# Attention feeding a PReLU layer on one Trainium2 core: the output weights loaded in eight pieces, one small load put later, the work between two blocks re-ordered

## The chip, the cores and the metric

The kernel runs on one core of one Trainium2 chip. The metric is the device time in microseconds (us) of one execution. The profile also gives the span from the first to the last instruction on the core, which is somewhat shorter than the device time: in the profiled execution of the kernel before, the device time was 279.78 us and the span 278.0 us.

Five engines work side by side and wait for each other through semaphores: TensorE (PE in the profile; its weight loads are PEld), VectorE (DVE), ScalarE (ACT), GpSimd (POOL) and SyncE (SP). Loads and stores are DMAs which an engine issues and which run on their own.

## The reference, cut to what matters

Eight batches of 576 tokens, eight heads of 64 features. The attention has no softmax; it is followed by a normalisation over each head's 64 features, and then by two matrix products with a PReLU between them, over all 4608 tokens.

```python
# q, k, v: (8 batches, 8 heads, 576 tokens, 64); w_in: (512, 2048); w_out: (2048, 512)
kv  = einsum('bhsd,bhse->bhde', k, v)
o   = einsum('bhsd,bhde->bhse', q, kv)
rms = sqrt(mean(o * o, axis=-1, keepdims=True) + 1e-06)
x   = (o / rms * g_norm)            # laid out as (4608 tokens, 512)
h   = x @ w_in
g   = maximum(h, 0) + alpha * minimum(h, 0)
out = g @ w_out                     # float32
```

## The kernel before

The tokens are worked on in nine blocks of 512 (`w` = 0 to 8). A batch has 576 tokens, so block 1 takes the last 64 tokens of batch 0 and the first 448 of batch 1, and block 2 the last 128 of batch 1 and the first 384 of batch 2.

A block's first product is made in 16 groups of 128 hidden features. Each group is four matmuls of 512 columns into one PSUM bank; ScalarE (`m_sb`) and VectorE (`gt`) read the bank, and only then can another group write it. The second product of block 0 is made directly, in 64 matmuls of 512 columns (`y_mm`: four token tiles `a`, sixteen feature groups `g`). From block 1 on it is made from seven products of half-sized matrices instead of eight, in 112 matmuls of 256 columns; it needs sums of parts of w_out (`w_sum`) and of the activations (`s_sum`), which VectorE makes.

The attention of the next block is woven into the current one. The stretch between the last group of block 0 and the first of block 1 is called stage two here: it holds most of block 0's second product, the attention of batch 1, and the sums of w_out.

```python
    def load_rem(b, nm):                      # the last 64 tokens of a batch
        nc.gpsimd.dma_start(out=buf_of(b, nm)[0:REM, 0 if nm == "v" else TPP, :, :],
                            in_=srcs[nm][b, :, MAIN:S, :].rearrange("h s d -> s h d"))
    # load_main(b, nm): the first 512 tokens into a stage tile; regroup() copies them to bufs
    def load_batch(b, names=("k", "v", "q")):
        for nm in names:
            load_rem(b, nm)
            load_main(b, nm)
    ...
    def load_w_out(i):                        # i = 0..3, 512 rows of w_out each
        t = w_p.tile([P, GW, D_MODEL], FP16, name=f"w_out_sb{i}")
        nc.gpsimd.dma_start(
            out=t[:], in_=moe_w_out[i*GW*P : (i+1)*GW*P, :].rearrange("(g p) m -> p g m", p=P))
    ...
    for i in range(len(IN_CUTS) - 1):
        load_w_in(i)
    load_batch(1, ("k",))
    load_w_out(0)
    load_batch(1, ("q",))
    load_w_out(1)
    load_batch(1, ("v",))
    load_w_out(2)
    load_w_out(3)
    ...
    # step_t: transposes of q (5 matmuls a pair of heads, then one copy to qt_sb by ScalarE)
    # step_kv: k'v of a pair (5 matmuls, then kv_sb by VectorE)
    # step_ot: q.kv of a pair and its square (ScalarE);  ssq_mm: sum of squares (PE), then
    #          the reciprocal root (ScalarE);  norm: xt (VectorE), the input of the next block
    ...
    load_batch(2, ("q", "k", "v"))
    ... # first three groups of block 0
    for g in range(3, NF):
        m1_group(0, g, {3: S_POOL, 4: O_POOL, 5: O_POOL, 6: Q_POOL}.get(g))
        if g == 14:
            regroup(1, "k", 0, H)
            for nm in ("k", "q"):
                nc.vector.memset(bufs[0][nm][REM:P, TPP, :, :], 0.0)
            for t in qt_sb:
                nc.vector.memset(t[:, :, 0:PAD], 0.0)
                nc.vector.memset(t[:, :, PAD + S : PAD + S + PAD], 0.0)
    ys = {}     # a = 3 in the bank of ps_y, a = 2, 0, 1 in the banks h0, h1, h2 of the groups
    ...
    regroup(1, "q", 0, H)
    for a in (3, 2, 0, 1):
        y_run(a, range(0, 4))
    w_sum(1, 0)
    for j, pool in enumerate((S_POOL, Q_POOL, O_POOL, O_POOL)):
        step_t(1, j, pool)
    for a in (2, 0, 1):
        y_run(a, range(4, 8))
    w_sum(1, 1)
    step_kv(1, 0)
    step_kv(1, 1, Q_POOL)
    ... # the rest of stage two; see the diff
    store_engines[0] = (nc.sync,)
    ...
    QT_AT = {False: {7: (0, 1), 9: (2, 3), 11: (4,)}, True: {8: (0,), 10: (1,), 12: (2, 3, 4)}}

    def attention(w, u):        # woven into block w - 1, after its group u
        if W_ROW <= w < NW:     # W_ROW = 3
            for what, j in ATT_ROW[w == W_ROW].get(u, ()):
                if what != "kv" or w < B:
                    ROWS[what](w, j)          # "norm" ends with a DMA transpose x_rows -> xt on SP
            if w + 1 < B:
                dma_t(w + 1, QT_AT[w == W_ROW].get(u, ()))   # DMA transposes of q on SP
        ... # blocks 0 to 2 by ATT_1 and ATT_AT
```

Of the kernel before, what the change touches and what calls it, by code (L numbers as in the profile page):

```python
# [10 lines left out]
FP16 = mybir.dt.float16  # L11
# [6 lines left out]
def kernel(  # L18
# [11 lines left out]
    nc = tc.nc  # L30

    B, H, S, D = q.shape
# [3 lines left out]
    P = 128  # L36
# [70 lines left out]
    nc.vector.tensor_copy(out=mask16[:], in_=mask32[:])  # L107
    eps_t = const_p.tile([P, 1], FP32, name="eps_t")
    nc.vector.memset(eps_t[:], 1e-6)

    alpha_row = ysb_p.tile([P, D_MODEL], FP32, name="y_sb")
    nc.sync.dma_start(out=alpha_row[0:NF, 0:P], in_=moe_alpha[:].rearrange("(g p) -> g p", p=P))
# [55 lines left out]
    def regroup(b, nm, h0, h1, eng=None):  # L168
        dst = buf_of(b, nm)[:, 0:TPP, h0:h1, :].rearrange("p t h d -> p h t d")
        src = stages[b, nm][:, h0:h1, :, :]  # L170
        if eng is nc.scalar:
            nc.scalar.copy(out=dst, in_=src)
        else:
            (eng or nc.vector).tensor_copy(out=dst, in_=src)
# [48 lines left out]

    def load_w_out(i):
        t = w_p.tile([P, GW, D_MODEL], FP16, name=f"w_out_sb{i}")
        nc.gpsimd.dma_start(
            out=t[:],
            in_=moe_w_out[i * GW * P : (i + 1) * GW * P, :].rearrange("(g p) m -> p g m", p=P),
        )
        w_out_sb.append(t)  # L230

    def w_in_blk(c, g):
# [41 lines left out]
    def rows(b):  # L274
        return P0 if b == 0 else P

    def n_runs(b):
        return T0 if b == 0 else NT

    def pair_cols(b, nm, j):  # L280
        def f(t):
            n = rows(b)
            if nm == "v" and b == 0:
                h = 2 * j % HH
                return stages[b, nm, 2 * j // HH][0:n, h : h + 2, t, :]
# [7 lines left out]
    def step_t(b, j, pool=(ps_s, "s")):  # L293
        qs = pair_cols(b, "q", j)
        qt_ps = pool[0].tile([P, n_runs(b) * rows(b)], FP16, name="qt_ps", tag=pool[1])
        c = 0
        for t in range(n_runs(b)):
            n = rows(b)
            nc.tensor.matmul(
                out=qt_ps[:, c : c + n],  # L300
                lhsT=qs(t),
                rhs=ident16[0:n, 0:n],
                is_transpose=True,
                start=(t == 0),
                stop=(t == n_runs(b) - 1),
            )
            c += n
        qts[b, j] = qt_sb[b % 2][:, j, PAD : PAD + S]
        if b == 0 and j < 2:
            nc.vector.tensor_copy(out=qts[b, j], in_=qt_ps[:, 0:S])  # L310
        else:
            nc.scalar.copy(out=qts[b, j], in_=qt_ps[:, 0:S])

    PAD = P // 2
    qt_sb = [const_p.tile([P, NPAIR, PAD + S + PAD], FP16, name=f"qt_sb{i}") for i in range(2)]

    def dma_t(b, ts=tuple(range(NT))):
        qt = qt_sb[b % 2][:, :, PAD : PAD + S]
# [435 lines left out]
    h_turn[0] = 2  # L754
    for g in range(3, NF):
        m1_group(0, g, {3: S_POOL, 4: O_POOL, 5: O_POOL, 6: Q_POOL}.get(g))
        if g == 14:
            regroup(1, "k", 0, H)
            for nm in ("k", "q"):
                nc.vector.memset(bufs[0][nm][REM:P, TPP, :, :], 0.0)  # L760
            for t in qt_sb:
                nc.vector.memset(t[:, :, 0:PAD], 0.0)
                nc.vector.memset(t[:, :, PAD + S : PAD + S + PAD], 0.0)


    ys = {}
# [3 lines left out]
    def y_run(a, gs):  # L770
        for g in gs:
            y_mm(ys[a], 0, a, g)
# [9 lines left out]
    w_sum(1, 1)  # L782
    step_kv(1, 0)
    step_kv(1, 1, Q_POOL)
    y_run(3, (4, 5))
    step_kv(1, 2)
    step_kv(1, 3, Q_POOL)
    step_ot(1, 0)
    y_run(3, (6,))
    step_ot(1, 1)  # L790
    y_run(3, (7,))
    y_run(2, (8,))
    ssq_mm(1, 0)
    norm(1, 0)
    y_run(2, (9, 10))
    ssq_mm(1, 1, Q_POOL)
    norm(1, 1)
    w_sum(2, 0)
    w_sum(4, 0)
    y_run(2, (11,))  # L800
    y_run(0, (8, 9, 10))
    step_ot(1, 2)
    y_run(0, (11,))
    y_run(1, (8,))
    step_ot(1, 3)
    y_run(1, (9, 10))
    ssq_mm(1, 2)
    w_sum(2, 1)
    norm(1, 2)
    y_run(1, (11,))  # L810
    y_run(0, (12,))
    ssq_mm(1, 3, Q_POOL)
    norm(1, 3)
    regroup(2, "q", 0, H)
    w_sum(4, 1)
    w_sum(3, 0)
    w_sum(3, 1)
    y_run(0, (13, 14, 15))
    y_out(ys[0], 0, 0)
    y_run(2, range(12, 16))  # L820
    y_out(ys[2], 0, 2)
    y_run(1, range(12, 16))
    y_out(ys[1], 0, 1)
    store_engines[0] = (nc.sync,)
    h_turn[0] = 0
    h_tags[0] = ("h0", "h1", "h2")
# [24 lines left out]
            ATT_AT.setdefault(3 * j + at, []).append((what, j))  # L851
    ATT_1 = {}
    for what, ats in (
        ("t", (0, 2, 4, 7)), ("kv", (4, 5, 6, 8)), ("ot", (7, 7, 11, 12)), ("ssq", (8, 10, 12, 13))
    ):
        for j, at in enumerate(ats):
            ATT_1.setdefault(at, []).append((what, j))
# [35 lines left out]

    REG_AT = {9 + 2 * j: (("k", j),) for j in range(NPAIR)}

    Y3_AT = [(8, 8), (8, 8), (8, 8), (8, 9), (9, 9), (9, 10), (10, 10), (10, 10), (10, 11), (11, 11), (11, 12), (12, 12), (12, 13), (13, 14), (14, 16), (16, 16)]
    REG_2 = {0: (("k", 0), ("k", 1)), 1: (("k", 2), ("k", 3))}

    for w in range(1, NW):
        if w + 2 < B:  # L900
            load_gated(w + 2)
        for u in range(NF):
            if w >= W_ROW - 1 and u in R_FIRST:
                y_read(w - 1, R_FIRST[u])
            m1_group(w, G_ORDER[u])
            if w == W_ROW - 1:
                scale_w_in(G_ORDER[u])
            if w > 1:
# [81 lines left out]
```

## Time and profile before

| | |
|---|---|
| device time, median of 3 runs | 280.06 us (278.78 to 281.0) |
| span of the profiled execution | 278.0 us |
| TensorE busy | 269.5 us, 1928 matmuls |
| VectorE busy | 231.1 us |
| ScalarE busy | 155.6 us |
| one matmul of 512 columns, as profiled | 379 ns |
| granted TensorE clock | 0.999 |

The profile counts an engine as busy from an instruction's start to its end. Matmuls overlap in the array, so their durations do not add up: what a matmul takes of TensorE's time is the distance between one start and the next where nothing is waited for. In the chain view four matmuls of 512 columns take 0.86 us, so one takes 0.216 us; five transposes of 128 columns take 0.28 us, so one takes 0.056 us.

First matmuls of the blocks, from the trace: 15.28 us (block 0), 47.29 (1), 66.80 (2), 95.72 (3), 124.52 (4), 152.81 (5), 180.86 (6), 209.13 (7), 236.06 (8). The last group of block 0 begins at 28.76, the first matmul of block 0's second product at 29.62. Stage two is the stretch from 29.6 to 47.3.

The names in the profile are those of the program's tiles: `vst` and `vsb` are the main part and the last tokens of v, `qst` and `qsb` those of q; `y` is block 0's second product, `yX`, `yY`, `yZ` the later ones; `h_ps` is the first product. A wait such as "PE kv_ps <- DMA vst" says that TensorE stood idle before a matmul into `kv_ps` until a load of `vst` landed.

### The profile page before, as it was taken

Reading aid. Unit: us, or ns where it says so; the run is one execution under the profiler, and the core shown is the slowest. Engines: PE = TensorE matmul, PEld = TensorE weight load, DVE = VectorE, ACT = ScalarE, POOL = GpSimd, SP = SyncE. Lnnn points to the kernel's source line nnn. Section 1 sums busy time; section 2 is a strip of 40 time slices with the busy share of each in tenths; the row PEclk is TensorE's granted clock in tenths of the full one; section 3 lists DMA queues with packets and bytes.
Section 4 is the critical chain, followed back from the end, with each engine's and each line's share of the span. In section 5 each row is a group of like instructions: output and inputs, shape, how many; then the busy total and the mean of one; then the engine's idle time right before and its main releaser. Section 6 shows DMA issues by size and latency. Waiting matters only on the chain.

```text
span 278.0 us, 5178 instructions
## 1 busy us (share of the span) xinstructions
PE 269.5 (97%) x1928; PEld 173.2 (62%) x1928; DVE 231.1 (83%) x446; ACT 155.6 (56%) x284; POOL 81.9 (29%) x115
## 2 busy tenths in 40 slices
PE   7899999999999999999999999999999999999994
PEld 2444454555666676657666766676666666666784
DVE  5669829898789979997899889988998899887862
ACT  3567347789989846654565456545535554444210
POOL 8744432750913346226321831110111011000200
PEclk9999999999999999999999999999999999999999
DMA  8999999999998589986995699520222023201123
GB/s 161 195 207 197 196 203 191 203 136 166 123 170 116 124 112 143 152 184 91 167 186 118 102 167 185 126 78 0 78 75 78 0 77 78 75 0 40 70 84 113
DMA packets 86557, 34.53 MB, mean 124 GB/s; under 512 B 58740, under 2 KB 84868, under 8 KB 86532
## 3 DMA queue, kind: packets, MB, share of 16 engines
q0 software_dynamic: 57424, 24.35, 68.1%
q1 hardware_dynamic: 28212, 8.90, 16.3%
q10 hardware_dynamic: 896, 0.95, 1.1%
q8 instruction: 15, 0.25, 0.4%
q14 instruction: 10, 0.08, 0.1%
HBM read 36.71 MB, written 9.44 MB: 166 GB/s over the span
## 4 chain that ended last, share of the span: by engine, by line
PE 79%; DMA 13%; DVE 4%; issue 2%; ACT 1%; POOL 1%; DVEq 0%; POOLq 0%
PE h_ps L456 37%; PE yY L615 14%; PE yX L615 9%; PE yZ L615 9%; DMA vst<-in_v_dram 5%; DMA w_in_sb<-in_moe_w_in_dram 5%; PE kv_ps L332 3%; PE y L481 2%; DMA qst<-in_q_dram 2%; PE or_ps L398 2%; DVE gt L467 1%; DMA xt<-x_rows 1%; PE ot_ps L354 1%; ACT m_sb L463 1%; PE ssq_ps L370 1%
## 5 line engine op out<-in xcount | busy, mean ns | idle before, releaser
L456 PE MATMUL h_ps<-xt,w_in_sb 128*128 128x512 f16 x576 | 145.2, 379 | 0.8 <-DMA xt<-x_rows 0.6
L463 ACT ACTIVATE m_sb<-h_ps 128x512 f32<-128x512 f32 x144 | 86.1, 598 | 83.5 <-PE h_ps L456 81.9
L467 DVE SCALAR_TENSOR_TENSOR gt<-m_sb,beta_sb,h_ps 128x512 f16<-128x512 f32 x144 | 106.6, 743 | 25.9 <-ACT m_sb L463 23.1
L456 PEld LDWEIGHTS <-w_in_sb 128*128 128x128 f16 x576 | 54.5, 98 | 43.6 <-DMA xt<-x_rows 1.2
L492 POOL DMA_DIRECT2D out_dram<-y_sb x36 | 22.8, 636 | 144.0 <-DVE y_sb L659 43.6
L615 PEld LDWEIGHTS <-s 128*128 128x128 f16 x512 | 50.1, 98 | 19.8 <-DVE s L567 0.6
L615 PEld LDWEIGHTS <-gt 128*128 128x128 f16 x384 | 37.6, 98 | 14.8
L615 PE MATMUL yY<-wsum,s 128*128 128x256 f16 x256 | 36.5, 273 | 0.3 <-DVE s L567 0.3
L615 PE MATMUL yX<-w_out_sb,gt 128*128 128x256 f16 x256 | 35.1, 273 | 0.0
L154 POOL DMA_DIRECT2D qst<-in_q_dram x20 | 17.7, 917 | 1.8 <-DVE gt L467 1.8
L615 PE MATMUL yZ<-wsum,s 128*128 128x256 f16 x128 | 17.6, 273 | 0.0
L615 PE MATMUL yZ<-w_out_sb,s 128*128 128x256 f16 x128 | 17.6, 273 | 0.0
L615 PE MATMUL yY<-wsum,gt 128*128 128x256 f16 x128 | 17.6, 273 | 0.0
L481 PE MATMUL y<-w_out_sb,gt 128*128 128x512 f16 x64 | 17.0, 379 | 0.6 <-DVE gt L467 0.6
L413 ACT ACTIVATE sq_sb<-or_ps 128x512 f16<-128x512 f32 x24 | 14.3, 597 | 5.7 <-PE or_ps L398 4.6
L436 DVE TENSOR_TENSOR x_rows<-or_ps,rstd_r 128x512 f16<-128x512 f32 x24 | 16.4, 682 | 0.0
L419 DVE TENSOR_REDUCE ssq_r<-sq_sb 128x8 f32<-128x512 f16 x24 | 16.3, 678 | 0.0
L567 DVE TENSOR_TENSOR s<-s,gt 128x512 f16<-128x512 f16 x32 | 13.5, 422 | 0.5
L565 DVE TENSOR_TENSOR s<-gt 128x512 f16<-128x512 f16 x32 | 13.3, 417 | 0.1
L571 DVE TENSOR_TENSOR s<-gt,s 128x512 f16<-128x512 f16 x32 | 13.2, 416 | 0.0
L340 DVE TENSOR_TENSOR kv_sb<-kv_ps,mask 128x128 f16<-128x128 f32 x32 | 8.2, 284 | 5.6 <-PE kv_ps L332 5.6
L332 PEld LDWEIGHTS <-ksb 128*128 128x128 f16 (+1 forms) x164 | 10.5, 98 | 3.7 <-DMA vst<-in_v_dram 1.0
(80 smaller groups left out, 249.5 us busy)
## 6 DMA issues: line engine op xcount, KB each, us to landing
out_dram<-y_sb POOLq DMA_DIRECT2D x16, 256.0 KB, 2.7
kst<-in_k_dram POOLq DMA_DIRECT2D x7, 512.0 KB, 8.7
vst<-in_v_dram POOLq DMA_DIRECT2D x7, 512.0 KB, 10.8
qst<-in_q_dram POOLq DMA_DIRECT2D x20, 128.0 KB, 8.5
w_out_sb<-in_moe_w_out_dram POOLq DMA_DIRECT2D x4, 512.0 KB, 15.9
w_in_sb<-in_moe_w_in_dram POOLq DMA_DIRECT2D x3, 512.0 KB, 12.0
out_dram<-y_sb SPq DMA_DIRECT2D x5, 256.0 KB, 2.2
qst<-in_q_dram POOLq DMA_DIRECT2D x2, 512.0 KB, 16.1
```

Source lines behind the costliest of these rows:

```text
L154: nc.gpsimd.dma_start(out=st[:, t, :, :], in_=srcs["q"][b, :, t * P : (t + 1) * P, :].rearrange("h p d -> p h d"),)
L332: nc.tensor.matmul(out=kv_ps[:], lhsT=ks(t), rhs=vs(t), start=(t == 0), stop=(t == n_runs(b) - 1),)
L413: nc.scalar.activation(out=sq[:], in_=o_ps[:], func=AF.Square)
L419: nc.vector.tensor_reduce(out=ssq[:], in_=sq[:].rearrange("p (h d) -> p h d", h=H), axis=mybir.AxisListType.X, op=ALU.add,)
L436: nc.vector.tensor_tensor(out=xr[:], in0=o_ps[:].rearrange("p (h d) -> p h d", h=H), in1=rstd[:].unsqueeze(2).to_broadcast([P, H, D]), op= ...
L456: nc.tensor.matmul(out=h_ps[:], lhsT=w_in_blk(c, g), rhs=xts[w][:, c, :], start=(c == 0), stop=(c == NC - 1),)
L463: nc.scalar.activation(out=m_sb[:], in_=h_ps[:], func=AF.Relu, scale=-1.0)
L467: nc.vector.scalar_tensor_tensor(out=gts[w, i][:, r, :], in0=m_sb[:], scalar=beta_sb[:, g : g + 1], in1=h_ps[:], op0=ALU.mult, op1=ALU.add,)
L481: nc.tensor.matmul(out=y[:], lhsT=gt_cols(w, g, a * P, (a + 1) * P), rhs=w_out_blk(g), start=(g == 0), stop=(g == NF - 1),)
L492: engs[store_turn[0] % len(engs)].dma_start(out=dst, in_=src)
L567: nc.vector.tensor_sub(out=t[:], in0=sums[w, 1, k][:], in1=a11)
L615: nc.tensor.matmul(out=bank, lhsT=lhs, rhs=rhs, start=fresh, stop=(c == NK - 1), skip_group_check=True,)
```

## The change

The change has these parts.

1. w_out is loaded in eight pieces of 256 rows instead of four of 512, so that the first half of a tile can be used before the second has landed.
2. The load of the last 64 tokens of batch 1's q goes from before w_out's second quarter to behind the last one. These tokens belong to block 2. Their transposes leave `step_t(1, j)`, which now makes four transposes a pair and copies 512 columns instead of 576; a new `step_t_rem` makes the four left-over ones at the end of stage two, with one copy.
3. The clears of `qt_sb` go to the start of the program, those of two buffers of k and q into stage two, and the regrouping of batch 1's k behind the last group of block 0.
4. Stage two's matmuls are put in another order, with more of the second product ahead of the first step that needs v.
5. In block 1 some attention steps (`ATT_1`), the left-over token tile of block 0 (`Y3_AT`) and two activation sums are placed at other groups; the third pair of sums (`s_sum(1, w, 2)`) is made one step earlier, at the end of block 1 and behind block 2's first group.
6. From block 3 on, the DMA transpose of q's fourth run goes from group 9 to group 11, behind the last transpose of the block's x.

```diff
+    qt_sb = [...]                      # allocated and its pads cleared near the program's start
+    for t in qt_sb:
+        nc.vector.memset(t[:, :, 0:PAD], 0.0)
+        nc.vector.memset(t[:, :, PAD + S : PAD + S + PAD], 0.0)
 ...
     def load_w_out(i):
-        nc.gpsimd.dma_start(out=t[:], in_=moe_w_out[i * GW * P : (i + 1) * GW * P, :]...)
+        for r in range(0, GW, GW // 2):
+            g = i * GW + r
+            nc.gpsimd.dma_start(out=t[:, r : r + GW // 2, :],
+                in_=moe_w_out[g * P : (g + GW // 2) * P, :]...)
 ...
     load_w_out(0)
-    load_batch(1, ("q",))
+    load_main(1, "q")
     load_w_out(1)
     load_batch(1, ("v",))
     load_w_out(2)
     load_w_out(3)
+    load_rem(1, "q")
 ...
-        if g == 14:
-            regroup(1, "k", 0, H)
-            ... memsets of bufs[0] and of qt_sb
+    regroup(1, "k", 0, H)
 ...
     for j, pool in enumerate((S_POOL, Q_POOL, O_POOL, O_POOL)):
         step_t(1, j, pool)
-    for a in (2, 0, 1):
-        y_run(a, range(4, 8))
+    y_run(2, (4,)); y_run(0, (4,))
     w_sum(1, 1)
+    y_run(2, (5,)); y_run(3, (4,)); y_run(0, (5,)); y_run(1, (4,)); y_run(0, (6,))
+    for nm in ("k", "q"):
+        nc.vector.memset(bufs[0][nm][REM:P, TPP, :, :], 0.0)
+    y_run(2, (6,)); y_run(3, (5,)); y_run(1, (5, 6)); y_run(2, (7,)); y_run(0, (7,))
+    y_run(1, (7,)); y_run(3, (6,))
     step_kv(1, 0)
     step_kv(1, 1, Q_POOL)
-    y_run(3, (4, 5)); step_kv(1, 2); step_kv(1, 3, Q_POOL)
-    step_ot(1, 0); y_run(3, (6,)); step_ot(1, 1); y_run(3, (7,)); y_run(2, (8,))
-    ssq_mm(1, 0); norm(1, 0); y_run(2, (9, 10)); ssq_mm(1, 1, Q_POOL); norm(1, 1)
-    w_sum(2, 0); w_sum(4, 0); y_run(2, (11,)); y_run(0, (8, 9, 10)); step_ot(1, 2)
-    y_run(0, (11,)); y_run(1, (8,)); step_ot(1, 3); y_run(1, (9, 10)); ssq_mm(1, 2)
-    w_sum(2, 1); norm(1, 2); y_run(1, (11,)); y_run(0, (12,)); ssq_mm(1, 3, Q_POOL)
-    norm(1, 3); regroup(2, "q", 0, H); w_sum(4, 1); w_sum(3, 0); w_sum(3, 1)
-    ... rest of y, y_out
+    y_run(3, (7,)); step_ot(1, 0); step_kv(1, 2); step_ot(1, 1); y_run(2, (8,))
+    step_kv(1, 3, Q_POOL); ssq_mm(1, 0); y_run(0, (8,)); y_run(2, (9,)); norm(1, 0)
+    ssq_mm(1, 1, Q_POOL); norm(1, 1); w_sum(2, 0); y_run(0, (9,)); y_run(1, (8, 9)); w_sum(4, 0)
+    y_run(2, (10, 11)); step_ot(1, 2); y_run(1, (10,)); step_ot(1, 3); y_run(0, (10,))
+    ssq_mm(1, 2); norm(1, 2); w_sum(2, 1); y_run(2, (12,)); y_run(0, (11,)); ssq_mm(1, 3, Q_POOL)
+    y_run(1, (11,)); w_sum(3, 1); norm(1, 3); y_run(2, (13,)); y_run(0, (12,))
+    regroup(2, "q", 0, H); y_run(0, (13,)); w_sum(3, 0); ... rest of y, y_out, w_sum(4, 1)
+    step_t_rem(1, Q_POOL)
 ...
-    ATT_1: t at (0, 2, 4, 7), kv at (4, 5, 6, 8), ot at (7, 7, 11, 12), ssq at (8, 10, 12, 13)
+    ATT_1: t at (0, 2, 4, 8), kv at (5, 5, 7, 7), ot at (7, 7, 11, 12), ssq at (8, 10, 13, 13)
 ...
-    QT_AT = {False: {7: (0, 1), 9: (2, 3), 11: (4,)}, True: {8: (0,), 10: (1,), 12: (2, 3, 4)}}
+    QT_AT = {False: {7: (0, 1), 9: (2,), 11: (3, 4)}, True: {8: (0,), 10: (1,), 12: (2, 3, 4)}}
 ...
     for w in range(1, NW):
         for u in range(NF):
             m1_group(w, G_ORDER[u])
+            if w < 3 and (w, u) in ((1, NF - 1), (2, 0)):
+                s_sum(1, w, 2)
 ...
-                for k in {5: (0,), 7: (1,)}.get(u, ()):
+                for k in {4: (0,), 7: (1,)}.get(u, ()):
                     s_sum(1, 1, k)
                     s_sum(1, 2, k)
 ...
-                if u < 2:              # w == 2
-                    s_sum(1, u + 1, 2)
```

More of the change, by code (lines that the diff above doesn't have):

```diff
@@ L109 @@
     nc.vector.memset(eps_t[:], 1e-6)
+    PAD = P // 2
+    qt_sb = [const_p.tile([P, NPAIR, PAD + S + PAD], FP16, name=f"qt_sb{i}") for i in range(2)]
+    for t in qt_sb:
+        nc.vector.memset(t[:, :, 0:PAD], 0.0)
+        nc.vector.memset(t[:, :, PAD + S : PAD + S + PAD], 0.0)
     alpha_row = ysb_p.tile([P, D_MODEL], FP32, name="y_sb")
@@ L225, in load_w_out @@
         t = w_p.tile([P, GW, D_MODEL], FP16, name=f"w_out_sb{i}")
[L226 to L229, printed above, removed]
+        for r in range(0, GW, GW // 2):
+            g = i * GW + r
+            nc.gpsimd.dma_start(
+                out=t[:, r : r + GW // 2, :],
+                in_=moe_w_out[g * P : (g + GW // 2) * P, :].rearrange("(g p) m -> p g m", p=P),
+            )
         w_out_sb.append(t)
@@ L291, in pair_cols, with transposes, step_t, step_t_rem @@
         return f
[L293 to L298, printed above, removed]
+    def transposes(qt_ps, c, b, j, ts):
+        n = rows(b)
+        for t in ts:
             nc.tensor.matmul(
                 out=qt_ps[:, c : c + n],
-                lhsT=qs(t),
+                lhsT=pair_cols(b, "q", j)(t),
                 rhs=ident16[0:n, 0:n],
                 is_transpose=True,
-                start=(t == 0),
-                stop=(t == n_runs(b) - 1),
+                start=(c == 0),
+                stop=True,
+                skip_group_check=True,
             )
             c += n
-        qts[b, j] = qt_sb[b % 2][:, j, PAD : PAD + S]
[L309 to L315, printed above, removed]
+    def step_t(b, j, pool=(ps_s, "s")):
+        ts = range(TPP if b == 1 else n_runs(b))
+        n = min(S, len(ts) * rows(b))
+        qt_ps = pool[0].tile([P, len(ts) * rows(b)], FP16, name="qt_ps", tag=pool[1])
+        transposes(qt_ps, 0, b, j, ts)
+        qts[b, j] = qt_sb[b % 2][:, j, PAD : PAD + S]
+        eng = nc.vector.tensor_copy if b == 0 and j < 2 else nc.scalar.copy
+        eng(out=qts[b, j][:, 0:n], in_=qt_ps[:, 0:n])
+    def step_t_rem(b, pool):
+        qt_ps = pool[0].tile([P, NPAIR * P], FP16, name="qt_ps", tag=pool[1])
+        for j in range(NPAIR):
+            transposes(qt_ps, j * P, b, j, (TPP,))
+        nc.scalar.copy(
+            out=qt_sb[b % 2][:, :, PAD + MAIN : PAD + S],
+            in_=qt_ps[:].rearrange("p (j n) -> p j n", j=NPAIR)[:, :, 0:REM],
+        )
     def dma_t(b, ts=tuple(range(NT))):
@@ L756 @@
         m1_group(0, g, {3: S_POOL, 4: O_POOL, 5: O_POOL, 6: Q_POOL}.get(g))
-        if g == 14:
-            regroup(1, "k", 0, H)
[L759 to L763, printed above, removed]
+    regroup(1, "k", 0, H)
     ys = {}
@@ L779 @@
         step_t(1, j, pool)
-    for a in (2, 0, 1):
-        y_run(a, range(4, 8))
+    y_run(2, (4,))
+    y_run(0, (4,))
     w_sum(1, 1)
+    y_run(2, (5,))
+    y_run(3, (4,))
+    y_run(0, (5,))
+    y_run(1, (4,))
+    y_run(0, (6,))
+    for nm in ("k", "q"):
+        nc.vector.memset(bufs[0][nm][REM:P, TPP, :, :], 0.0)
+    y_run(2, (6,))
+    y_run(3, (5,))
+    y_run(1, (5, 6,))
+    y_run(2, (7,))
+    y_run(0, (7,))
+    y_run(1, (7,))
+    y_run(3, (6,))
     step_kv(1, 0)
     step_kv(1, 1, Q_POOL)
-    y_run(3, (4, 5))
+    y_run(3, (7,))
+    step_ot(1, 0)
     step_kv(1, 2)
+    step_ot(1, 1)
+    y_run(2, (8,))
     step_kv(1, 3, Q_POOL)
[L788 to L792, printed above, removed]
     ssq_mm(1, 0)
+    y_run(0, (8,))
+    y_run(2, (9,))
     norm(1, 0)
-    y_run(2, (9, 10))
     ssq_mm(1, 1, Q_POOL)
@@ L798 @@
     w_sum(2, 0)
+    y_run(0, (9,))
+    y_run(1, (8, 9,))
     w_sum(4, 0)
-    y_run(2, (11,))
-    y_run(0, (8, 9, 10))
+    y_run(2, (10, 11,))
     step_ot(1, 2)
-    y_run(0, (11,))
[L804 to L809, printed above, removed]
+    y_run(1, (10,))
+    step_ot(1, 3)
+    y_run(0, (10,))
+    ssq_mm(1, 2)
+    norm(1, 2)
+    w_sum(2, 1)
+    y_run(2, (12,))
+    y_run(0, (11,))
+    ssq_mm(1, 3, Q_POOL)
     y_run(1, (11,))
+    w_sum(3, 1)
+    norm(1, 3)
+    y_run(2, (13,))
     y_run(0, (12,))
-    ssq_mm(1, 3, Q_POOL)
-    norm(1, 3)
     regroup(2, "q", 0, H)
-    w_sum(4, 1)
[L816 to L820, printed above, removed]
+    y_run(0, (13,))
+    w_sum(3, 0)
+    y_run(0, (14,))
+    y_run(2, (14,))
+    y_run(0, (15,))
+    y_out(ys[0], 0, 0)
+    w_sum(4, 1)
+    y_run(2, (15,))
     y_out(ys[2], 0, 2)
-    y_run(1, range(12, 16))
+    y_run(1, (12, 13, 14, 15,))
     y_out(ys[1], 0, 1)
+    step_t_rem(1, Q_POOL)
     store_engines[0] = (nc.sync,)
@@ L853 @@
     for what, ats in (
-        ("t", (0, 2, 4, 7)), ("kv", (4, 5, 6, 8)), ("ot", (7, 7, 11, 12)), ("ssq", (8, 10, 12, 13))
+        ("t", (0, 2, 4, 8)), ("kv", (5, 5, 7, 7)), ("ot", (7, 7, 11, 12)), ("ssq", (8, 10, 13, 13))
     ):
@@ L894 @@
     REG_AT = {9 + 2 * j: (("k", j),) for j in range(NPAIR)}
-    Y3_AT = [(8, 8), (8, 8), (8, 8), (8, 9), (9, 9), (9, 10), (10, 10), (10, 10), (10, 11), (11, 11), (11, 12), (12, 12), (12, 13), (13, 14), (14, 16), (16, 16)]
+    Y3_AT = [(8, 8), (8, 8), (8, 8), (8, 9), (9, 10), (10, 10), (10, 10), (10, 10), (10, 11), (11, 12), (12, 13), (13, 13), (13, 13), (13, 14), (14, 16), (16, 16)]
     REG_2 = {0: (("k", 0), ("k", 1)), 1: (("k", 2), ("k", 3))}
```

## The prediction

> **What bounds the kernel now.** I read the head of the page and its chain first, then the list of TensorE's waits, then the timelines around each wait.
>
> ```profile
> span 278.0 us, 5178 instructions
> PE 269.5 (97%) x1928; PEld 173.2 (62%) x1928; DVE 231.1 (83%) x446; ACT 155.6 (56%) x284; POOL 81.9 (29%) x115
> PE 79%; DMA 13%; DVE 4%; issue 2%; ACT 1%; POOL 1%; DVEq 0%; POOLq 0%
> ```
>
> TensorE carries 79% of the chain, and the 13% of DMA lie almost wholly before 38 us. The busy share of 97% alone doesn't show that TensorE is full, since matmul durations overlap; I therefore took the distances between matmul starts in the trace and compared them with 0.216 us for 512 columns, 0.108 for 256 and 0.056 for 128 or fewer. From 15.3 us on, few starts come late. The waits view has most of them:
>
> ```profile
> PE y L481 <- DVE gt L467: 0.6, 1, 0.6
> PE h_ps L456 <- DMA xt<-x_rows: 0.6, 1, 0.6
> PE kv_ps L332 <- DMA vst<-in_v_dram: 0.4, 1, 0.4
> PE yY L615 <- DVE s L567: 0.3, 1, 0.3
> ```
>
> Counted by starts these are 0.76 us lost before the matmul at 32.97, 0.75 at 124.52, 0.53 at 38.08 and 0.45 at 72.30; smaller ones are 0.22 at 42.74 (a step_ot that waits for a norm), 0.09 at 40.59, and 0.19 at 95.72. So the change can save about three microseconds of 278 at most in the part it touches: the work itself, and so the number of matmuls, stays.
>
> The first two stage-two waits, in the timeline (start, duration, engine):
>
> ```profile
> 30.25 0.82 DVE L174 COPY ksb<-kst 128x2048 f16<-128x2048 f16 x1
> 31.17 0.27 DVE L760 MEMSET ksb<- 64x256 uint32 x1
> 31.44 0.27 DVE L760 MEMSET qsb<- 64x256 uint32 x1
> 31.79 0.17 DVE L762 MEMSET qt_sb<- 128x128 uint32 x1
> ...
> 32.21 0.17 DVE L763 MEMSET qt_sb<- 128x128 uint32 x1
> 32.29 0.63 DVE L467 SCALAR_TENSOR_TENSOR gt<-m_sb,beta_sb,h_ps 128x512 f16<-128x512 f32 x1
> ...
> 32.97 1.02 PE L481 MATMUL y<-w_out_sb,gt 128*128 128x512 f16 x4 [0.59 <-DVE gt L467]
> ...
> 38.08 0.40 PE L332 MATMUL kv_ps<-vst,ksb 128*128 128x128 f16 x4 [0.36 <-DMA vst<-in_v_dram]
> ```
>
> The evacuation of group 15 stands behind a regrouping and six clears on VectorE, although ScalarE finished its part at 30.42. The fourth y tile needs that group's bank, so TensorE stands still. The second wait is for v, and the chain says how long that load was on its way:
>
> ```profile
> 24.21 13.82 DMA vst<-in_v_dram
> 38.03 0.05 issue
> ```
>
> It was issued 13.82 us before it landed: it stood in the queue behind others. The semaphore times in the trace give the landings one after the other: w_out first quarter 29.33, q's last tokens 29.75, q's main part 32.38, w_out second quarter 34.92, v's last tokens 35.36, v's main part 38.03, w_out 40.55 and 43.10, then batch 2's q at 46.35, k at 49.41 and v at 52.53. A quarter of w_out or a main part takes 2.5 to 2.7 us, a load of last tokens 0.4.
>
> **What the Trainium skill says.** "DMA: Bandwidth & Descriptors", section "Anatomy of one DMA — SWDGE (gpsimd) path", estimates about 2 us of fixed time a DMA, most of it the receipt, plus bytes over 436 GB/s. If that were paid in line, four more DMAs would cost 8 us; the landings above follow each other at 0.4 us for the small loads, so this trace shows it overlapped when a queue is full. The same page, section "Bandwidth", advises pieces of 1 MiB or more; an eighth of w_out is 0.5 MiB of fp32, and I expect the queue's depth to hide that too. "SBUF — State Buffer" warns of "DVE blocks DMA": some VectorE instructions keep GpSimd from writing descriptors. The trace doesn't show it at the head: three load issues between 2.1 and 4.6 us, partly beside clears, took 0.67 to 0.68 us like those without. "Perfetto Trace Analysis", section "Identifying the Most-Contended Engine", says that TensorE's busy share is a poor measure because matmuls are pipelined; the 379 ns profiled against 216 ns between starts agree.
>
> **The change part by part.**
>
> *Clears and regrouping.* The evacuation of group 15 now follows its ScalarE part at 30.42 and ends near 31.2. TensorE reaches the fourth y tile at 29.62 + 12 x 0.216 = 32.21: no wait, 0.76 us gained. The four clears at the head cost VectorE 4 x 0.14 = 0.6 us; it idles 0.81 us before the cast at 5.08, so nothing moves.
>
> *Last tokens of q.* v's main part no longer has them ahead: 38.03 - 0.42 = 37.6 us. The queue keeps a backlog, so four more issues don't starve it. GpSimd waits before each issue for the landing of the load eight issues earlier (w_out's second issue, 18.49, follows the landing of the fourth w_in piece before it, 18.20). With more pieces v's issue moves behind the landing at 24.10, to about 24.9, ten microseconds before the queue gets to it.
>
> *Order.* Sixteen y matmuls end at 33.08. The regrouped q is there: main part 32.38 - 0.42 = 31.96, plus 0.68, is 32.65. Sixteen transposes (0.90) end at 33.98, fifteen y matmuls (3.24) at 37.22; the halves of w_out's second quarter land near 33.2 and 34.5, before their use. That a reader waits only for its own half I infer from kv of batch 0, which began at 12.49 on a tile whose second load landed at 12.98. Then 0.4 us of waiting remain until 37.66, 0.42 earlier than now. From there the old work to the end was 9.21 - 0.31 of waits = 8.90; three y matmuls fewer (0.65) and four transposes more (0.23) leave 8.48. One wait stays likely: step_ot of the third and fourth pair needs the PSUM bank of norms. Along the chain ssq, root, norm (1.93 us from ssq to the next step_ot in the old trace, the second norm 0.70 later) the fourth is possible at 42.33 and TensorE is there at 42.09; with small change I put 0.3 us. Block 1 begins at 37.66 + 8.48 + 0.3 to 0.4 = 46.5 instead of 47.29: **0.75 us gained**.
>
> *Block 1.* Its matmuls are the same. VectorE now has little lead: second norm 42.3, then five w_sums (0.65 to 0.69 each), two norms (0.74), q's regrouping (0.68, landed 46.35) and the first gt at 48.7 against 48.98 now. Group 3 needs that bank after 49.45; TensorE gets there at 49.7. The first transpose of batch 2 needs q regrouped at 47.43 and comes at 47.40. Both are tight; I take 0.1 us off.
>
> *Third activation sum.* The wait at 72.30 is for a sum that stands behind two gts on VectorE, which wait for ScalarE. Made a group earlier, it is ready. ScalarE is nearly full in this stretch: its regrouping of k ends at 72.23 and kv uses it at 72.98, so 0.75 us of slack takes up the 0.45. **0.35 to 0.45 us gained.**
>
> *Transposes of q.*
>
> ```profile
> 117.68 1.70 SPq L441 DMA_TRANSPOSE xt<-x_rows  x1
> 119.49 2.54 SPq L322 DMA_TRANSPOSE qt_sb<-qst  x2
> 122.12 1.23 SPq L441 DMA_TRANSPOSE xt<-x_rows  x1
> ```
>
> The last x rows were ready at 119.21 (end of the norm), but SP was held by two q transposes. With one ahead, x starts about 1.25 us sooner and lands near 123.2 instead of 124.48. TensorE would be there at 124.52 - 0.75 = 123.77, so the wait should go, unless the earlier blocks' gain (1.1 us) brings TensorE there before the transposes: norm and issue move with the block, the transposes' own 1.25 us don't. **0.6 us gained.** In later blocks no wait of this kind is seen, so nothing is gained there.
>
> Sum: 0.75 - 0.1 + 0.4 + 0.6 = 1.65 us, with 0.1 to 0.2 for the smaller waits about 1.8. After block 2 TensorE has hardly a wait, so a gain reaches the end. 280.06 - 1.8 = 278.3.
>
> **Rivals.** *VectorE takes over at the seam.* If block 1 is held by the first gt and q's regrouping instead of by TensorE's order, only VectorE's 0.3 us come through. For: those two margins of about 0.2 us and none. Against: from group 3 on, banks come free 0.4 to 1.7 us before use in the old trace. Then the gain is 1.3 us, time 278.8. *The eight pieces slow the queue.* If each of four more DMAs cost 0.3 us in line, v would be 0.6 later and batch 2's v 1.2 later than 52.53, into kv of batch 2; stage two would gain nothing: about 279.5. For: the fixed cost; against: the 0.4 us loads. *Gains are swallowed by the next wait.* Block 2 is bound by ScalarE at its start and block 4 by the x transposes; if both keep their time, stage two's gain is lost again there and only the 0.6 us of block 4's transpose order stays: 279.5.
>
> **Range and chances.** The median of three before lies in 278.78 to 281.0, so a median is uncertain by some 0.7 us, and my gain by as much: 0.5 to 2.5. Together: 277.0 to 280.0 eight times in ten. 2% would be 5.6 us, more than all the waits found, so faster by that gets 0.02; slower by that needs a new wait of over 5 us, such as a starved queue, also 0.02.
>
> **What would show it.** Right: no wait of y for gt near 32; kv at 37.6 to 37.7; first matmul of block 1 at 46.4 to 46.6, block 2 about 0.7 earlier than 66.80, block 3 about 1.1 earlier than 95.72; the x transpose of block 4 behind one q transpose, and no wait there. Wrong: v's landing after 38; waits in block 1 for gt or for q's regrouping; a new wait in block 3 or later; or a span shorter by under 0.8 us.

## The result, and the profile after

| | before | after |
|---|---|---|
| device time, median of 6 runs each | 279.90 us | 278.16 us (277.73 to 278.53) |
| ratio, 95% interval | | 0.9936 (0.9909 to 0.9963) |
| span of the profiled execution | 278.0 us | 276.6 us |
| first matmul of block 0 | 15.28 | 16.27 |
| first y matmul of stage two | 29.62 | 30.62 |
| first matmul of block 1 | 47.29 | 47.05 |
| of block 2 | 66.80 | 66.56 |
| of block 3 | 95.72 | 95.03 |
| of block 4 | 124.52 | 123.09 |
| last matmul's end | 274.49 | 273.05 |

The kernel after is faster by 0.6%, between 0.4% and 0.9%. The head of its page and its chain:

```profile
span 276.6 us, 5185 instructions
PE 269.4 (97%) x1928; PEld 173.4 (63%) x1928; DVE 231.4 (84%) x446; ACT 155.5 (56%) x285; POOL 84.4 (31%) x119
PE 91%; DVE 3%; DMA 2%; ACT 1%; issue 1%; ACTq 0%; DVEq 0%; POOLq 0%
```

The matmuls are the same 1928. TensorE's part of the chain has grown from 79% to 91%, because the chain no longer leads through a load up to 38 us: v is not what stage two waits for in this profile. Of the four waits of TensorE shown in the prediction none is in the list any more. The list now holds only waits of the program's first 12 us; these are two of its five lines:

```profile
PE kv_ps L348 <- DMA vst<-in_v_dram: 1.1, 1, 1.1
PE ot_ps L370 <- DVE kv_sb L356: 0.3, 2, 0.2
```

The 1.1 us stand before the first kv of the whole program, at 7.96 us: the first load of v landed at 7.91 us here and at 6.98 in the profile before. So everything up to stage two runs about one microsecond later in this profile, and the gain of 1.44 us at the last matmul is the sum of a loss and larger gains. Between the starts in the table: head +0.99, stage two 17.67 to 16.43 = -1.24, block 2 28.92 to 28.47 = -0.45, block 3 28.80 to 28.06 = -0.74; the rest is the same to 0.02 us.

Stage two in the timeline after (start, duration, engine):

```profile
28.00 4.20 DVE L483 SCALAR_TENSOR_TENSOR gt<-m_sb,beta_sb,h_ps 128x512 f16<-128x512 f32 x5
...
30.62 3.62 PE L497 MATMUL y<-w_out_sb,gt 128*128 128x512 f16 x16
...
32.12 0.69 DVE L179 COPY ksb<-kst 128x2048 f16<-128x2048 f16 x1
...
34.97 3.40 PE L497 MATMUL y<-w_out_sb,gt 128*128 128x512 f16 x15
...
38.25 0.40 PE L348 MATMUL kv_ps<-vst,ksb 128*128 128x128 f16 x4
```

The five last evacuations now follow each other and end at 32.20; only then comes the regrouping, and sixteen y matmuls run without a stop. Fifteen more lead up to kv, which waits 0.05 us: v landed at 38.20.

The seam to block 1, where the prediction saw two tight places:

```profile
46.83 0.39 PE L304 MATMUL qt_ps<-ident,qsb 128*128 128x128 f16 x4
...
47.05 1.03 PE L472 MATMUL h_ps<-xt,w_in_sb 128*128 128x512 f16 x4
47.12 0.68 DVE L179 COPY qsb<-qst 128x2048 f16<-128x2048 f16 x1
...
47.92 0.44 PE L304 MATMUL qt_ps<-ident,qsb 128*128 128x128 f16 x5
...
48.92 0.74 DVE L483 SCALAR_TENSOR_TENSOR gt<-m_sb,beta_sb,h_ps 128x512 f16<-128x512 f32 x1
```

Batch 2's q is regrouped at 47.80, and the transposes that read it begin at 47.92; the first gt begins at 48.92 and the fourth group, which needs its bank, at 50.20. Neither holds TensorE here. SP's part at the end of block 3:

```profile
116.30 1.42 SPq L457 DMA_TRANSPOSE xt<-x_rows  x1
117.82 1.21 SPq L338 DMA_TRANSPOSE qt_sb<-qst  x1
119.12 1.22 SPq L457 DMA_TRANSPOSE xt<-x_rows  x1
120.44 1.22 SPq L338 DMA_TRANSPOSE qt_sb<-qst  x1
```

One transpose of q stands ahead of x's last one instead of two; x lands at 122.46 and block 4 begins at 123.09 without a wait.

The third activation sum, in block 2, before and after:

```profile
71.83 0.42 DVE L567 TENSOR_TENSOR s<-s,gt 128x512 f16<-128x512 f16 x1
...
72.30 0.28 PE L615 MATMUL yY<-wsum,s 128*128 128x256 f16 x1 [0.29 <-DVE s L567]
```

```profile
69.05 0.42 DVE L583 TENSOR_TENSOR s<-s,gt 128x512 f16<-128x512 f16 x1
...
71.18 0.71 PE L631 MATMUL yY<-wsum,s 128*128 128x256 f16 x5
```

Before, the sum ended at 72.25 and the last of five matmuls waited for it until 72.30. After, it ends at 69.47 and the five run without a stop.

### The profile page after: what moved, and what is told of

Same layout as the page of the kernel before. It is cut to its first block, busy times and chain, and to the rows that moved or that the text cites. A ratio compares the mean times of both kernels' runs of the same rounds, so it can differ in the third digit from the quotient of the medians.

```text
span 276.6 us, 5185 instructions
## 1 busy us (share of the span) xinstructions
PE 269.4 (97%) x1928; PEld 173.4 (63%) x1928; DVE 231.4 (84%) x446; ACT 155.5 (56%) x285; POOL 84.4 (31%) x119
## 4 chain that ended last, share of the span: by engine, by line
PE 91%; DVE 3%; DMA 2%; ACT 1%; issue 1%; ACTq 0%; DVEq 0%; POOLq 0%
PE h_ps L472 42%; PE yY L631 15%; PE yZ L631 10%; PE yX L631 10%; PE y L497 4%; PE kv_ps L348 3%; DMA vst<-in_v_dram 2%; PE or_ps L414 2%; DVE gt L483 1%; PE qt_ps L304 1%; PE ot_ps L370 1%; ACT m_sb L479 1%; DVE xt L395 1%; PE ssq_ps L386 1%; ACT rstd L388 1%
## 5 line engine op out<-in xcount | busy, mean ns | idle before, releaser
L472 PEld LDWEIGHTS <-w_in_sb 128*128 128x128 f16 x576 | 54.6, 98 | 42.7 <-issue 1.0
L631 PEld LDWEIGHTS <-gt 128*128 128x128 f16 x384 | 37.6, 98 | 14.8
L581 DVE TENSOR_TENSOR s<-gt 128x512 f16<-128x512 f16 x32 | 13.4, 418 | 0.0
```

Of the source, the lines that this page charges most:

```text
L472: nc.tensor.matmul(out=h_ps[:], lhsT=w_in_blk(c, g), rhs=xts[w][:, c, :], start=(c == 0), stop=(c == NC - 1),)
L631: nc.tensor.matmul(out=bank, lhsT=lhs, rhs=rhs, start=fresh, stop=(c == NK - 1), skip_group_check=True,)
```

## The experiments

A profile is one execution, so a wait in it can be chance. Each experiment below is told with its time against the kernel before on the same chip and with the waits of its own profile, counted by the distance between TensorE's starts. The length of stage two ("stage two took") is from the first y matmul to the first matmul of block 1.

**The clears back from the start.**

```diff
-    for t in qt_sb: ... memsets     # at the program's start
 ...
     for nm in ("k", "q"):           # in stage two
         nc.vector.memset(bufs[0][nm][REM:P, TPP, :, :], 0.0)
+    for t in qt_sb: ... memsets
```

> The kernel after, with the four clears of qt_sb back from the program's start to stage two (beside the two other clears there). In the profiled run of the kernel after, the first load of v landed at 7.91 us instead of 6.98 and the first matmul of block 0 began at 16.27 instead of 15.28. Theory A (chance from run to run): the clears at the start cost nothing; the time stays at 278.2 +- 0.5, and this run's first landing lies anywhere between 6.9 and 8. Theory B (the clears at the start slow the first loads): the first landing is back at 7.0, block 0 begins near 15.3, and the time is 277.2.

Measured: 278.62 us, ratio 0.9934 (0.9911 to 0.9956), the kernel after having 0.9936. The first load of v landed at 7.29 and block 0 began at 15.65. Over all profiles of this study, block 0 began on average at 15.53 us in the nine with the clears at the start (14.81 to 16.27) and at 15.71 in the five without (15.28 to 16.16). No cost of the clears at the start is to be seen, and the late head of the first profile was chance: the unchanged kernel below began block 0 at 15.61.

**q's transpose back.**

```diff
-    QT_AT = {False: {7: (0, 1), 9: (2,), 11: (3, 4)}, ...
+    QT_AT = {False: {7: (0, 1), 9: (2, 3), 11: (4,)}, ...
```

> The kernel after, with q's fourth DMA transpose back at group 9, ahead of the last transpose of x. Theory (SP's order is what held block 4): the last transpose of x in block 3 again stands behind two of q, TensorE waits 0.6 to 0.8 us for it before block 4, later blocks show no such wait, and the time is 278.8. Rival (that wait was a chance of the DMA's load in one run): no wait over 0.3 us at block 4, time 278.2.

Measured: 278.82 us, ratio 0.9943 (0.9915 to 0.9971). Block 4 began without a wait, although x's last transpose stood behind two of q; block 6 began 0.35 us late. The theory missed, and the order on SP alone is not what holds block 4. The time is the 278.8 that the theory named, but not by its wait, and the ratio can't be told from that of the kernel after. What came up instead is a wait for v in block 2, 0.50 us by starts:

```profile
69.97 0.38 PE L348 MATMUL kv_ps<-vst,ksb 128*128 128x128 f16 x4 [0.34 <-DMA vst<-in_v_dram]
```

**The third activation sum back.**

```diff
-            if w < 3 and (w, u) in ((1, NF - 1), (2, 0)):
-                s_sum(1, w, 2)
 ...
+                if u < 2:           # w == 2, at the end of the group
+                    s_sum(1, u + 1, 2)
```

> The kernel after, with the third pair of activation sums back where it was, at the ends of the first two groups of block 2. Theory: the wait of yY for VectorE's sum comes back, 0.4 to 0.5 us between TensorE's starts, and the span is longer by that, 278.6. Rival (block 2 is bound by ScalarE there, and the wait only moves to kv or to the next group): under 0.15 us difference, 278.2.

Measured: 278.69 us, ratio 0.9942 (0.9926 to 0.9958). The wait of yY for the sum didn't come back, but TensorE had lost 0.70 us just before, at 69.92, waiting for batch 3's v, which gave VectorE the time. So the undoing tells nothing of the sum. What does is that all four profiles with the old sum and without such a wait for v (the kernel before and three of its variants below) have the wait of 0.45 us, and none of those with the new one. These four also have the old order of stage two and block 1, so it is the lines shown above, not the comparison, that tie the wait to the sum; the early sum alone on the kernel before was not run.

**w_out in eight pieces, alone, on the kernel before.**

```diff
-        nc.gpsimd.dma_start(out=t[:], in_=moe_w_out[i * GW * P : ...])
+        for r in range(0, GW, GW // 2):
+            nc.gpsimd.dma_start(out=t[:, r : r + GW // 2, :], in_=...)
```

> The kernel before, with w_out alone in eight pieces. Theory (a full queue hides what a DMA costs by itself): the landings of the last piece of w_out and of batch 2's v move by under 0.2 us relative to the first loads, all waits of TensorE stay, time 279.9 +- 0.5. Rival (each further DMA costs some 0.3 us in line): v's main part lands 0.6 and batch 2's v 1.2 us later, and the time grows to 280.5 or more.

Measured: 280.62 us, ratio 1.0002 (0.9983 to 1.0021). From the landing of the first quarter of w_out to that of the last piece it takes 13.84 us, against 13.77 before; to batch 2's v 23.45 against 23.20. The queue hides nearly all of what four more DMAs cost. Block 4 began 1.59 us late in this profile, more than in the kernel before.

**The kernel after once more.** No edit.

> The kernel after once more, unchanged. It tells how far the waits of one profile are chance. Theory: the start of block 0 differs from the 16.27 us of the first profile by up to half a microsecond (other kernels with the same start had 15.74 and 15.98), stage two takes 16.4 us from its first y matmul to block 1, block 4 begins without a wait because x's last transpose stands behind one of q. Rival for block 4 (the wait there depends on when the loads of the block end, whatever SP's order): a wait of 0.3 us or more can show up here too.

Measured: 278.31 us, ratio 0.9927 (0.9900 to 0.9954). Block 0 began at 15.61, v landed at 37.82, kv waited 0.33 us for it, and stage two took 16.70 us. Block 4 began with a wait of 0.84 us:

```profile
123.48 1.02 PE L472 MATMUL h_ps<-xt,w_in_sb 128*128 128x512 f16 x4 [0.68 <-DVE gt L483]
```

The line names VectorE, whose gt ended at 123.45. In the kernel before, the same matmul began at 124.52 while that gt ran until 124.60, so it doesn't need it; it needs x, whose last transpose landed at 123.34. Batch 5's v had landed at 119.35. So the rival holds for block 4: with the new order, too, there can be a wait.

**The load of q's last tokens back.**

```diff
-    load_main(1, "q")
+    load_batch(1, ("q",))
     load_w_out(1)
 ...
-    load_rem(1, "q")
```

> The kernel after, with the load of the last tokens of batch 1's q back ahead of w_out's second quarter; their transposes stay late. Theory (v's landing sets stage two once the clears are out of the way): v lands 0.42 us later relative to the loads ahead of it, kv waits 0.2 to 0.5 us for it, stage two takes 16.6 to 16.9 us, time 278.6. Rival (only the order of stage two counts): no wait, 16.4 us, time 278.2.

Measured: 278.50 us, ratio 0.9937 (0.9915 to 0.9960), on the same chip as the kernel after once more. Stage two took 17.19 us:

```profile
37.53 0.40 PE L347 MATMUL kv_ps<-vst,ksb 128*128 128x128 f16 x4 [0.62 <-DMA vst<-in_v_dram]
```

The wait, 0.78 us by starts, is more than expected. In the kernel after once more kv waited 0.33 us already; there the first y matmul came 0.82 us later and w_out's first quarter landed 0.80 us later, but v only 0.34 us later. So with the load back v comes 0.46 us later in the line, and stage two takes 0.48 longer (17.19 against 16.70), as the theory has it. All nine profiles with the new order of stage two and w_out in halves follow one rule, to 0.05 us: block 1 begins 8.85 us after v lands or 16.37 us after the first y matmul, whichever is later (in the four with the old order it begins 9.17 to 9.26 us after v). The effect on the time, about 0.2 us, is within what these runs resolve, so it isn't shown by the time.

**w_out in four pieces, in the kernel after.**

```diff
-        for r in range(0, GW, GW // 2): ... two loads a tile
+        nc.gpsimd.dma_start(out=t[:], in_=...)
```

> The kernel after, with w_out in four pieces again. Theory (the new order needs the halves): y's ninth group waits for the whole third quarter of w_out, which lands near 40.0 and is wanted near 39.3, so stage two is 0.5 to 0.9 us longer, time 278.9. Rival (the pieces are idle detail, v sets the end): stage two 16.4 to 16.6 us, time 278.2.

Measured: 279.00 us, ratio 0.9958 (0.9944 to 0.9972), against 0.9927 for the kernel after on the same chip. Stage two took 17.76 us. Two y matmuls wait for a whole quarter:

```profile
34.66 3.40 PE L495 MATMUL y<-w_out_sb,gt 128*128 128x512 f16 x15 [0.34 <-DMA w_out_sb<-in_moe_w_out_dram]
...
40.30 0.38 PE L495 MATMUL y<-w_out_sb,gt 128*128 128x512 f16 x1 [0.73 <-DMA w_out_sb<-in_moe_w_out_dram]
```

By starts they are 0.51 and 0.89 us; the first, for the second quarter, was not expected. The pieces alone are worth nothing and cost nothing; the new order needs them.

**The clears and the regrouping alone, on the kernel before.**

```diff
     for g in range(3, NF):
         m1_group(0, g, ...)
-        if g == 14:
-            regroup(1, "k", 0, H) ... and six memsets
+    regroup(1, "k", 0, H)
 ...
     w_sum(1, 1)
+    ... six memsets
     step_kv(1, 0)
```

> The kernel before, with batch 1's k regrouped behind group 15 and all six clears behind the second sum of w_out; nothing else. Theory (two waits in a row, the later one counts): the wait of 0.76 us for the evacuation of group 15 is gone and the wait for v grows to 0.8 to 1.3 us; block 1 begins at v's landing plus 9.2 us as before, time 280.2, within 0.3 of the kernel before. Rival (the waits add up): the gain is 0.76 us, time 279.6.

Measured: 280.52 us, ratio 1.0000 (0.9975 to 1.0026). The wait for the evacuation is gone, and kv waits for v:

```profile
38.45 0.40 PE L332 MATMUL kv_ps<-vst,ksb 128*128 128x128 f16 x4 [0.46 <-DMA vst<-in_v_dram]
```

By starts 0.62 us, with 0.18 for w_out before it; the first y matmul was late in this profile (30.50), so v's wait is smaller than expected. Block 1 began 9.20 us after v's landing at 38.41. The theory holds: two waits in a row are not two gains.

**q's transpose alone, on the kernel before.**

```diff
-    QT_AT = {False: {7: (0, 1), 9: (2, 3), 11: (4,)}, ...
+    QT_AT = {False: {7: (0, 1), 9: (2,), 11: (3, 4)}, ...
```

> The kernel before, with q's fourth DMA transpose moved from group 9 to group 11 and nothing else. In the kernels with the old order, block 4 has begun with waits of 0.75, 0, 1.59 and 1.70 us, in those with the new order with 0, 0, 0.47, 0.84, 0 and 0. Theory (both SP's order and the end of the block's loads count; the new order is worth about 1 us when the loads end late): the wait before block 4 is under 0.6 us, the waits of stage two and block 2 stay, time 279.6. Rival (only the end of the loads counts): a wait of 1 us or more again, time 280.4.

Measured: 279.41 us, ratio 0.9981 (0.9968 to 0.9995): faster by 0.5 us, between 0.1 and 0.9. Block 4 began 0.17 us late; the other waits stayed (0.62 for gt, 0.35 for v, 0.45 for the sum). SP's list shows what changed:

```profile
119.17 1.21 SPq L322 DMA_TRANSPOSE qt_sb<-qst  x1
120.47 1.22 SPq L441 DMA_TRANSPOSE xt<-x_rows  x1
```

In the kernel before that last transpose of x was issued at 122.12. To see both influences I set, for all profiles but the two with stores on SP, the landing of batch 5's v in block 3 (us after block 3's first matmul) beside the wait before block 4:

| order of q's transposes | kernel | v lands after | wait before block 4 |
|---|---|---|---|
| old | q's transpose back | 22.28 | 0 |
| old | before | 23.63 | 0.75 |
| old | clears alone | 23.96 | 1.70 |
| old | pieces alone | 25.09 | 1.59 |
| new | block 1 woven as before | 22.45 | 0 |
| new | after | 22.58 | 0 |
| new | w_out in four pieces | 22.81 | 0 |
| new | q's last tokens back | 22.86 | 0 |
| new | q's transpose alone | 23.10 | 0.17 |
| new | clears back | 23.11 | 0 |
| new | third sum back | 24.00 | 0.47 |
| new | after once more | 24.77 | 0.84 |

As far as single profiles go, both count. With the loads over by 22.9 us there is no wait in either order (the old one has one such profile); between 23.6 and 24.0 us the old order waits 0.75 and 1.70, the new one 0.47. Why the loads of one and the same program end one or two microseconds earlier or later is open.

**Block 1 woven as before.**

```diff
-    kv at (5, 5, 7, 7), t at (0, 2, 4, 8), ssq at (8, 10, 13, 13); Y3_AT new; sums at group 4
+    kv at (4, 5, 6, 8), t at (0, 2, 4, 7), ssq at (8, 10, 12, 13); Y3_AT old; sums at group 5
```

> The kernel after, with block 1 woven as in the kernel before (attention steps, left-over token tile and first pair of sums at their old groups). Theory (block 1 starts earlier but batch 2's v doesn't land earlier, so its steps had to be put later): the first kv of batch 2, now at group 4, is reached near 51.9 and waits 0.5 to 1.0 us for v, block 1 takes 20.0 to 20.5 us instead of 19.5, time 278.9. Rival (the new weave is worth nothing): block 1 takes 19.5 to 19.6 us, time 278.2.

Measured: 278.78 us, ratio 0.9952 (0.9935 to 0.9970). Block 1 took 20.32 us instead of 19.51:

```profile
52.44 0.38 PE L348 MATMUL kv_ps<-vst,ksb 128*128 128x128 f16 x4 [0.65 <-DMA vst<-in_v_dram]
```

By starts that is 0.81 us, as the theory has it: batch 2's v landed at 52.40, and block 1, begun at 46.26, got to its kv too soon. Without the new weave stage two's gain would have been handed back here. That is read from the profile; the ratio, 0.9952, is not clear of the 0.9927 and 0.9936 of the kernel after, which was not run on this chip.

**Block 0's stores on SP.** The kernel after, with the six stores of stage two's output issued by SP.

```diff
-    store_engines = [(nc.gpsimd,)]
+    store_engines = [(nc.sync,)]
```

> The kernel after, with block 0's six output stores of stage two issued by SP instead of GpSimd. In four of the profiles with the new stage two, batch 3's v landed too late for kv in block 2 (waits of 0.28, 0.50, 0.70, 0.94 us). Theory (GpSimd's stores hold up the issue of batch 3's loads by some 3 us, so the queue runs dry): batch 3's v lands before 68 us, no wait for it in block 2, time 277.9. Rival (v is late because it shares the DMA engines with SP's transposes and stores): it lands as late, 278.2.

Measured: 280.17 us, ratio 1.0000 (0.9984 to 1.0017): the whole gain of the change is lost. Batch 3's v did land sooner, at 65.05, and block 2 had no wait for it, so that half of the theory holds. But batch 2's v, issued at 42.2 as ever, took 12.8 us instead of 10.5 in the kernel after, and block 1 waits for it:

```profile
46.15 3.10 SPq L508 DMA_DIRECT2D out_dram<-y_sb  x6
```

```profile
55.03 0.38 PE L348 MATMUL kv_ps<-vst,ksb 128*128 128x128 f16 x4 [1.78 <-DMA vst<-in_v_dram]
```

On GpSimd's queue the stores went behind that load, landing from 53.57 us on, after v at 53.06. SP's go beside it and take DMA time from it: in the DMA view of 50 to 52 us GpSimd's queue moved 0.14 MB and SP's 0.46, while from 48 to 49.5 us GpSimd's had moved 0.29 MB alone. But the edit also let GpSimd issue the next loads sooner, the first main part of batch 3's q at 48.47 instead of 53.63. Their small packets move beside v's last part: packets under 512 B number 77 from 50 to 52 us and 1805 from 52 to 54.6. How the 1.95 us that TensorE waits divide between stores and loads is open.

**Loads freed of q's last tokens.** As the last one, and from batch 4 on the last tokens of q are loaded behind v.

```diff
     def load_gated(b):
-        load_rem(b, "q")
+        if b == B_NAT: load_rem(b, "q")
         ...
         load_rem(b, "v"); load_main(b, "v")
+        if b > B_NAT: load_rem(b, "q")
```

> As the kernel with block 0's stores on SP, and from batch 4 on the last tokens of q are loaded behind v instead of first, since their load waits until the last q transpose of the batch before has read its buffer, and all loads behind it wait with it on GpSimd. Theory: the loads of blocks 2 to 5 are issued 3 to 5 us sooner, they end sooner than x's transposes want the DMA engines, and no block from 3 on begins with a wait for x over 0.2 us; time 277.6. Rival (x's transposes are held by other things than the loads' end): waits as in the kernel after, 278.0.

Measured: 279.96 us, ratio 0.9997 (0.9983 to 1.0010). Block 1 waits 2.03 us for batch 2's v again. The other half came out: batch 5's v landed 17.25 us after block 3's first matmul instead of 21.5 to 25.1 elsewhere, x's last transpose landed at 122.59, and block 4, at 124.72, had none to wait for; block 3 still began 0.28 us late. The time doesn't tell what this second edit is worth, since the stores hide it; it wasn't run without them.

## Why the prediction was right

The time was 278.16 us against 278.3 predicted and a range of 277.0 to 280.0. What each term became can be followed in single profiles only, while the time is a median.

*Signs and luck.* Two signs failed in the first profile after: v landed at 38.20, and a landing after 38 was to mean that the prediction is wrong; block 1 began at 47.05 instead of 46.4 to 46.6. Its head had started 0.99 us late. Once more and unchanged, the kernel had v at 37.82, block 1 at 46.66, block 2 0.63 and block 3 1.14 us earlier than before, close to the forecast, but 0.84 us of waiting before block 4, where none was forecast. At the last matmul the two profiles gain 1.44 and 0.96 us on the one profile before, less than the medians do (1.74 and 2.12). Single executions differ by as much as most of the terms, so that the median came within 0.2 us of the forecast is in part luck.

*Stage two as a whole.* Counted from the landing of the whole first quarter of w_out, which takes out how early the loads of an execution are, block 1 begins after 17.96 us in the kernel before, after 17.13 and 17.12 in the two profiles after. These 0.83 us, against 0.75 in the working, are 0.42 because v lands sooner and 0.41 because less is left to do once it is there. With 0.45 for the sum in block 2 and 0.5 for q's transpose alone that makes about 1.8 us, an estimate from those profiles and that one time; 1.8 was forecast. The new order, the late tokens and the early sum were not run one by one on the kernel before.

*Clears.* Right: no wait for gt near 32. The step called it "0.76 us gained", and alone (with the regrouping) it gains nothing (ratio 1.0000); the sum had rightly counted stage two only once, by v's landing.

*Last tokens of q.* v was to land at 37.6. It landed at 38.20 in the first profile after, whose loads were all late, and at 37.33 to 37.82 in the eight others that load q's last tokens late. Counted from the end of w_out's first quarter it is 8.28 us instead of 8.70: the 0.42 of the working. (The landing at 18.20 that the step names is that of the third of five w_in pieces; it is the load eight issues earlier, as the step says.)

*Order.* From the first y matmul to kv the working has 37.66 - 29.62 = 8.04 us with 0.44 of waiting; without it 7.60, measured 7.63 with 0.05 of waiting. From kv to block 1 it has 8.48 and 0.3 to 0.4; measured 8.80, with 0.22 for the step_ot that waits for a norm. Its size of the gain, 0.75 us, was too small for this pair of profiles (1.24) because TensorE came one microsecond later and v only 0.2 us later, so that the wait for v fell away. In the kernel after once more, with the head 0.66 us earlier, the wait for v is there (0.33). How the head and the load queue stand to each other varies from execution to execution, and the working took one profile's as fixed.

*Block 1.* The margins were judged rightly: 0.12 us between the regrouping of q and its use in the first profile after, and waits of 0.07 and 0.11 us for it in the kernel with the clears back and in the last experiment. The step said of the weave only that the matmuls are the same. That the weave keeps 0.81 us from being lost was not foreseen.

*Third sum.* 0.35 to 0.45 us: measured 0.45 in block 2. The slack that was to take it up was sought on ScalarE. The next wait was another one, batch 3's v: none in both profiles of the kernel after, but 0.28, 0.50, 0.70 and 0.94 us in four of its variants. Part of this gain is so given back in some executions.

*Transposes of q.* 0.6 us; 0.75 in the first pair, 0.5 (0.1 to 0.9) by the time of that edit alone. The mechanism stands only with its condition: it counts when the block's loads end late, and then the new order doesn't remove the whole wait.

*Rivals.* Eight pieces slowing the queue: no (1.0002). VectorE at the seam: no wait over 0.11 us. Gains swallowed by the next wait: in part, by the load of batch 3's v rather than by ScalarE.

## What to carry to other kernels

When an engine waits twice in a row, removing the first wait moves the time to the second; only the landing or release that ends last sets what the stretch is worth, so count the stretch once, from that. Once a stretch starts earlier while the loads do not, the consumers of the next loads have to be placed later, or the gain is handed back a block on. A small load delays every load behind it in the queue (here by 0.42 us). Moving stores to another queue, where they run beside a load instead of behind it, can cost more (here 1.95 us) than the wait that one set out to remove (at most 0.94).

## What the runs showed of the hardware that was not expected

The same six stores cost TensorE nothing when they stood behind batch 2's v in GpSimd's queue, and TensorE waited 1.95 us when SP issued them beside it: v took 12.8 us from issue to landing instead of 10.5. The next loads, which came sooner for it, have a part in this that was not separated.

DMA transposes that SP issued while a batch was being loaded landed only about when its last load did. In the kernel after, x's first transpose of block 3 was issued at 108.44 and landed at 117.74, batch 5's v landed at 117.61; in the kernel before 109.14, 119.50 and 119.35. In block 2 of the kernel before, once the block's last load had landed (86.47), x's transposes landed 2.3 to 2.5 us after their issue. In the last experiment, where the loads ended 4 to 8 us earlier in the block, the first transpose, issued 13.4 us into it as ever, landed 19.56 us into it, against 21.71 to 24.74 in the other thirteen profiles. So in this run the earlier end of the loads moved it, but didn't set it alone: it landed at 116.22, 2.3 us after v (113.92), elsewhere within 1.2 us of v. No run took the loads away, and what holds a transpose back is open.

The first load of the program landed between 6.38 and 7.91 us in fourteen profiles, issued at the same time, and the start of block 0 mostly moved with it.
